# Attention and expert layers on one core: the first pair's loads and start-up work put in another order, and a DMA pipe in the planner's model

## The chip, the core and the metric

The kernel runs on one core of a Trainium2 chip. The core has five engines that run their own instruction lists and wait for each other by semaphores: TensorE (PE, matrix products and transposes), VectorE (DVE), ScalarE (ACT), GpSimd (POOL) and SyncE (SP, which here issues almost all DMA transfers). The metric is the device time of one launch in microseconds (us); less is better. A smaller change of the median than about 0.2% (2.4 us) can't be told from none here.

## The reference, cut to what matters

```python
def _attn_ref(q, k, v):                      # q, k, v: (4, 8, 1152, 64)
    q_pool = q.reshape(B, H, S // 2, 2, D).mean(axis=3)          # 576 pooled rows per head
    scores = scale * np.matmul(q_pool, k.transpose(0, 1, 3, 2))  # 576 x 1152
    scores = scores - np.max(scores, axis=-1, keepdims=True)
    attn = np.exp(scores)
    attn = attn / (np.sum(attn, axis=-1, keepdims=True) + 1e-09)
    return np.matmul(attn, v)

x = attn_out.transpose(0, 2, 1, 3).reshape(2304, 512)
x = ((x @ w1) * (x @ w2) @ w3) @ w_out       # gated layer
logits = x @ w_gate                          # 8 experts; greedy assignment, 288 tokens each
out[mask] = np.maximum(x[mask] @ w1[e], 0.0) @ w2[e]
```

## The kernel before

The kernel has two halves. In the profiled execution the attention fills the first 512 us and the gated layer, the routing of tokens and the experts fill the rest. All products are made in fp32 quality from pairs of fp32r numbers: a value is split into a high part (a cast) and a low part (the value less its high part), and two or three products are summed.

**Tiling of the attention.** Two heads of a batch make a pair; there are 16 pairs. Of each pair the 2 x 576 pooled rows of q are cut into 9 tiles of 128 rows (`tile_ops`, j = 0 to 8): 0 to 3 belong to the first head, 5 to 8 to the second, and tile 4 holds 64 rows of each. For each tile TensorE makes the scores in three pieces of 384 columns (L590, `s<-kst,qst`, two PSUM banks in turn), VectorE copies each piece to SBUF and keeps its minimum (L600, `p<-s`), ScalarE takes the exponential of the whole row (L605), TensorE transposes it back in three groups of three (L614, `pt<-ident,p`), ScalarE or GpSimd makes the high part `p_hi` and VectorE or GpSimd the low part `p_lo`, and `pv` multiplies with v (L664).

**Preparation of a pair.** `prepare_q` loads q (`qr`), adds neighbouring rows (`qs`, L443), transposes and scales (`qT`), splits into `qH` and `qL`, and moves both with eight DMAs inside SBUF to `qst` (`move`, L399). `prepare_k` loads k (`kr`), transposes, splits into `kH` and `kL`, and moves them to `kst`, one buffer for each head. `prepare_v` loads v (`vr`) and splits it (`vhl`). For tile 4 the 64 x 64 blocks `dH` and `dL` stand in for `qst`. For the first pair there is a short way: q is loaded in three groups (`g` 0 to 2), k of the first head is loaded by itself (`k`, L517) and transposed straight into `kst`, and `both` writes half of `qst` without a move.

**What sets the order.** Nothing is issued where it stands in the code. Each step is an `Op` with a cost per engine, a priority and dependences; `Sched.run` plays the whole program through in a model (each engine does the ready op with the lowest priority number next; an op that can run on several engines goes to the one that takes it first) and emits the instructions in order of their model start. The chip then works off each engine's list strictly in that order. A DMA is an op on the queue engine: `dur` is the issue, and `lat` the fixed time from issue to landing. An op's `slack` holds it back for so long after it is ready.

**Before the scheduler.** `routing_consts` makes the constants of the routing (names `rc_...`, needed only after 500 us) straight away: POOL writes number patterns into a spare tile of `xT`, and 27 small DVE instructions make the constants from them. Then `attention` clears parts of `dH` and `dL` with eight DVE memsets (L386, L387). Both stand ahead of everything else in DVE's list.

Of the kernel before, what the change touches and what calls it, by code (L numbers as in the profile page):

```python
# [344 lines left out]
def attention(nc, tc, sch, pool, prep, s_pt, s_s, ident, xT, rsum, q, k, v):  # L345
# [69 lines left out]
    def prepare_q(p, pr):  # L415
# [1440 lines left out]
```

## Time and profile before

| | |
|---|---|
| median of 3 runs | 1190.95 us (1189.04 to 1191.3) |
| the profiled execution | 1188.21 us |
| its span, first to last instruction | 1186.4 us |
| mean granted clock of TensorE | 0.991 of full speed |
| busy share of the span: PE, DVE, ACT, POOL | 97%, 79%, 60%, 44% |

The profiled execution is 2.74 us shorter than the median, and 0.83 us shorter than the fastest of the three runs. Its own time is 1.8 us more than its span. A busy share is a mean over both halves; the attention alone reads differently, as the windows below show.

### The profile page before, as it was taken

The numbers are of one execution on the slowest core, as the hardware profiler recorded it, in microseconds if no ns is written. First come the engines' busy times: TensorE is split into PE (matmuls) and PEld (weight loads), VectorE is DVE, ScalarE is ACT, GpSimd is POOL, SyncE is SP. The second block draws the span as 40 slices with busy tenths as digits, with TensorE's granted clock in tenths as the row PEclk, the third lists the DMA queues.
The fourth block names the chain that finished last, engine by engine and source line by source line (L and its number), as shares of the span: only waits on it lengthen the run. The fifth ranks groups of instructions, "written<-read, shape, count | busy, mean of one in ns | idle before, by whom it ended". The sixth has DMA issues, their size and how long they took to land.

```text
span 1186.4 us, 24411 instructions
## 1 busy us (share of the span) xinstructions
PE 1148.2 (97%) x8401; PEld 1089.1 (92%) x8401; DVE 934.9 (79%) x2955; ACT 706.7 (60%) x1499; POOL 517.0 (44%) x584
## 2 busy tenths in 40 slices
PE   6999999999999999999999999999999899999996
PEld 5999999999999999989999999977778889999996
DVE  7899999999999999998777775468767878877541
ACT  6787888888888888864433344323223455555530
POOL 4466666666656666610000000123444439987110
PEclk9999999999999999999999999999999899999998
DMA  9587676666676654124456660355111565556510
GB/s 215 143 172 156 151 159 145 148 156 157 156 154 149 150 115 106 57 73 155 178 171 193 201 198 22 122 192 171 38 46 45 149 212 182 195 176 198 187 54 21
DMA packets 114539, 168.05 MB, mean 142 GB/s; under 512 B 47543, under 2 KB 77758, under 8 KB 114414
## 3 DMA queue, kind: packets, MB, share of 16 engines
q1 hardware_dynamic: 111246, 157.05, 49.0%
q0 software_dynamic: 3168, 9.44, 2.6%
q8 instruction: 66, 1.08, 0.4%
q14 instruction: 59, 0.48, 0.1%
HBM read 104.87 MB, written 22.61 MB: 107 GB/s over the span
## 4 chain that ended last, share of the span: by engine, by line
PE 83%; DVE 10%; DMA 3%; issue 1%; SPq 1%; ACT 1%; POOL 0%; DVEq 0%; POOLq 0%; ACTq 0%
PE pb L113 40%; PE s L590 13%; PE pt L614 7%; PE pt L664 6%; PE pt L113 6%; PE s L664 6%; PE s L614 4%; DVE pt L113 2%; DMA u<-in_moe_w_dram 1%; DVE ul L113 1%; DVE p L600 1%; PE pt L543 1%; DVE cv_v L113 1%; DVE p_lo L648 0%; PE pt L479 0%
## 5 line engine op out<-in xcount | busy, mean ns | idle before, releaser
L600 DVE TENSOR_SCALAR_CACHE_REDUCE p<-s 128x384 f32<-128x384 f32 x432 | 230.0, 551 | 35.6 <-PE pt L614 12.2
L590 PE MATMUL s<-kst,qst 128*128 128x384 f32 x768 | 200.0, 360 | 6.9 <-DVE p L600 3.4
L605 ACT ACTIVATE p<-p,mn 128x1152 f32<-128x1152 f32 x144 | 181.1, 1258 | 25.2 <-DVE mn L603 23.1
L113 POOL TENSOR_TENSOR x2l<-hraw,x2h 128x512 fp32r<-128x512 f32 x36 | 47.4, 1323 | 291.0 <-PE pt L113 254.3
L113 PE MATMUL pb<-xhi,wh 128*128 128x288 f32 x512 | 155.9, 305 | 1.2 <-ACT wh L113 1.2
L113 PE MATMUL pb<-xhi,wl 128*128 128x288 f32 x512 | 151.0, 295 | 1.4 <-POOL wl L113 1.2
L113 PE MATMUL pb<-xlo,wh 128*128 128x288 f32 x512 | 150.7, 294 | 0.0
L590 PEld LDWEIGHTS s<-kst,qst 128*128 128x128 f32 x768 | 123.8, 191 | 13.1 <-DVE p L600 8.1
L614 PE MATMUL pt<-ident,p 128*128 128x128 f32 x879 | 132.5, 273 | 0.3 <-ACT p L605 0.3
L648 DVE TENSOR_TENSOR p_lo<-pt,p_hi 128x384 fp32r<-128x384 f32 x230 | 124.6, 551 | 0.9 <-ACT p_hi L331 0.9
L331 ACT ACTIVATE p_hi<-pt 128x384 fp32r<-128x384 f32 x230 | 106.6, 493 | 13.5 <-PE pt L614 11.3
L614 PEld LDWEIGHTS pt<-ident,p 128*128 128x128 f32 x879 | 107.3, 141 | 4.3 <-ACT p L605 0.5
L113 PEld LDWEIGHTS pb<-xhi,wh 128*128 128x128 f32 x512 | 96.3, 188 | 2.6 <-ACT wh L113 1.6
L113 PEld LDWEIGHTS pb<-xhi,wl 128*128 128x128 f32 x512 | 96.2, 188 | 1.8 <-POOL wl L113 1.4
L341 POOL TENSOR_TENSOR p_lo<-praw,p_hi 128x384 fp32r<-128x384 f32 x96 | 97.0, 1019 | 0.4
L113 PEld LDWEIGHTS pb<-xlo,wh 128*128 128x128 f32 x512 | 96.3, 188 | 0.0
L113 DVE SCALAR_TENSOR_TENSOR cv_v<-cv_raw,cv_v 128x512 int32<-128x512 int32 (+1 forms) x120 | 83.7, 705 | 5.6 <-ACT cv_raw L113 4.5
L113 POOL TENSOR_TENSOR ul<-u,uh 128x512 fp32r<-128x512 f32 x64 | 81.3, 1300 | 12.0 <-ACT uh L113 10.5
L335 POOL CAST p_hi<-praw 128x384 fp32r<-128x384 f32 x96 | 47.6, 506 | 82.2 <-ACT praw L331 81.9
L113 ACT ACTIVATE uh<-u 128x512 fp32r<-128x512 f32 x128 | 73.7, 625 | 14.7 <-DMA u<-in_moe_w_dram 13.7
L113 PE MATMUL pb<-ehh,uh 128*128 128x288 f32 x256 | 78.6, 307 | 0.0
L113 PE MATMUL pb<-exh,uh 128*128 128x288 f32 x248 | 77.2, 311 | 0.0
(317 smaller groups left out, 3177.4 us busy)
## 6 DMA issues: line engine op xcount, KB each, us to landing
u<-in_moe_w_dram SPq DMA_DIRECT2D x64, 512.0 KB, 3.7
cv_raw<-in_moe_w_dram SPq DMA_DIRECT2D x32, 512.0 KB, 4.0
vr<-in_v_dram SPq DMA_DIRECT2D x32, 288.0 KB, 5.5
kr<-in_k_dram SPq DMA_DIRECT2D x32, 288.0 KB, 5.9
kst<-kH SPq DMA_DIRECT2D x31, 288.0 KB, 4.1
kst<-kL SPq DMA_DIRECT2D x31, 288.0 KB, 5.0
qr<-in_q_dram SPq DMA_DIRECT2D x15, 576.0 KB, 6.3
w3t<-wg SPq DMA_DIRECT2D x16, 512.0 KB, 3.5
```

The source lines that it names most:

```text
L113: return f(*[x.get() if isinstance(x, Lazy) else x for x in a], **{n: x.get() if isinstance(x, Lazy) else x for n, x in k.items()})
L331: nc.scalar.activation(out, in_, AF.Copy)
L335: nc.gpsimd.tensor_copy(out, in_)
L341: (nc.vector if eng == "DVE" else nc.gpsimd).tensor_tensor(out, a, b, op=OP.subtract)
L543: nc.tensor.transpose(ps.tile[:, a * 128:(a + 1) * 128], r[:, 3 * c + a, :, :].rearrange("p h d -> p (h d)"), ident)
L590: nc.tensor.matmul(ps.tile[:, :384], a[:, :], b[:, cs], start=(n == 0), stop=(n == len(passes) - 1))
L600: sch.op("DVE", c_dve(384), lambda ps=ps, c=c, cs=cs: nc.vector.tensor_scalar(t[:, cs], ps.tile[:, :384], 1.0, BIG, op0=OP.mult, op1=OP.mi ...
L605: sch.op("ACT", c_act(S, psum=False, acc=True), lambda: nc.scalar.activation(t, t, AF.Exp, bias=mn[:, 3:4], scale=-1.0, accum_out=sm[0][:, ...
L614: nc.tensor.transpose(ps.tile[:, a * 128:(a + 1) * 128], t[:, b * 128:(b + 1) * 128], ident)
L648: sch.op("DVE", c_dve(384), lambda view=view, src=src: nc.vector.tensor_tensor(view(lo), src(), view(hi).bitcast(F32), op=OP.subtract), us ...
L664: nc.tensor.matmul(ps.tile[:, :n], vt[:, t, :, :], src[half][:, t, off:off + n], start=(half == 0 and t == 0), stop=(half == 1 and t == NT ...
```

## The change

1. `routing_consts` hands its 27 DVE instructions to the scheduler as a chain of ops with priority 60 and a hold of 100 us. The number patterns on POOL stay at the start. `spare_read` keeps the last pair from writing the spare tile ahead of them.
2. The eight memsets of `dH` and `dL` go from DVE to POOL.
3. 14 transposes of the identity into the four `pt` banks stand at the head of PE's list (`WARM`).
4. The loads of `k` and of the first `vr` are issued on ACT's DMA queue, and q group 1 directly after group 0 on SP's.
5. `Sched` gets a `pipe` for the attention's transfers: a transfer lands no earlier than the one before it in the model plus its own size's time, so `lat` is no longer fixed. The first loads' slack now holds too (`pend` starts at `o.slack`), and there are new priorities and costs (`QG1`, `K_FIRST`, `KR_LATE`, `K_PIPE`).

```diff
@@ Sched.op, Sched.run
-    def op(self, engine, dur, fn, r=(), w=(), prio=0.0, lat=None, after=(), takes=None, uses=(), slack=0.0):
+    def op(self, engine, dur, fn, r=(), w=(), prio=0.0, lat=None, after=(), takes=None, uses=(), slack=0.0, pipe=None):
         o = Op()
-        o.slack = slack
+        o.slack, o.pipe = slack, pipe
...
-                    heapq.heappush(pend[e], (0.0, o.idx))
-        t, done = 0.0, 0
+                    heapq.heappush(pend[e], (o.slack, o.idx))
+        t, done, landed = 0.0, 0, 0.0
...
                 end = free[e] = t + o.alts[e]
+                if o.pipe is not None:
+                    landed = max(end + 1200.0, landed) + o.pipe
+                    o.lat = landed + 500.0 - end
@@ attention
-            nc.vector.memset(t[0:64, 64:128].bitcast(F32), 0.0)
-            nc.vector.memset(t[64:128, 0:64].bitcast(F32), 0.0)
+            nc.gpsimd.memset(t[0:64, 64:128].bitcast(F32), 0.0)
+            nc.gpsimd.memset(t[64:128, 0:64].bitcast(F32), 0.0)
...
-        sch.op("DMA", 650, lambda: nc.sync.dma_start(dst.bitcast(F32), src.bitcast(F32)), r=r, w=w, prio=pr, lat=2000)
+        sch.op("DMA", 650, lambda: nc.sync.dma_start(dst.bitcast(F32), src.bitcast(F32)), r=r, w=w, prio=pr, lat=2000, pipe=pipe)
@@ prepare_q
-                   w=[(kq, g) for g in range(3)], prio=pr, lat=3200, slack=SLACK)
+                   w=[(kq, g) for g in range(3)], prio=pr if p > 1 else -4.5, lat=3200, slack=SLACK * (p > 1), pipe=PIPE * 590)
...
-                    w=[(kqs, s_) for s_ in range(slot, slot + 2 * (s1 - s0), 2)], prio=pr)
+                    w=[(kqs, s_) for s_ in range(slot, slot + 2 * (s1 - s0), 2)], prio=(pr, QG1, QD1)[g] if first else pr)
...
-                        "p (s h d) -> p h s d", s=2, h=2)[:, 0], 128, [], key[:2], key[2:], pr + 2 * g + y, -0.0625)
+                        "p (s h d) -> p h s d", s=2, h=2)[:, 0], 128, [], key[:2], key[2:], pr + 0.02 * y, -0.0625)
@@ prepare_k, prepare_v
-            sch.op("DMA", 475, lambda r=r: nc.sync.dma_start(r, dram(k, 0, [[NT * D, 128], [1, NT * D]])), w=[kr], prio=pr, lat=2600)
+            sch.op("ACT", 475, lambda r=r: nc.scalar.dma_start(r, dram(k, 0, [[NT * D, 128], [1, NT * D]])), w=[kr], prio=pr, lat=2600, pipe=PIPE * 295, slack=K_FIRST)
...
-            sch.op("DMA", 475, lambda dst=dst, src=src: nc.sync.dma_start(dst, src), w=[(kr, h)], prio=pr + 2 * h, lat=2600, slack=SLACK)
+            sch.op("DMA", K_LOAD, lambda dst=dst, src=src: nc.sync.dma_start(dst, src), w=[(kr, h)], prio=pr + 2 * h, lat=2600,
+                   slack=SLACK + KR_LATE * (p == 1), pipe=PIPE * 295 * K_PIPE)
...
+        early = p == h == 0
+        sch.op("ACT" if early else "DMA", 475, lambda: (nc.scalar if early else nc.sync).dma_start(
+            r, dram(v, base, [[NT * D, 128], [1, NT * D]])), w=[kr], prio=-88 if early else pr, lat=2600, slack=2 * K_FIRST if early else SLACK, pipe=PIPE * 295)
@@ routing_consts
+    def dve(n, fn):
+        o = sch.op("DVE", c_dve(n), fn, prio=RC_PRIO, lat=0.0, slack=0.0 if made else RC_SLACK)
+        o.deps.update(made[-1:])
+        made.append(o)
...
-    nc.vector.tensor_scalar(tri, jp, 0.0, None, op0=OP.is_le)
+    dve(128, lambda: nc.vector.tensor_scalar(tri, jp, 0.0, None, op0=OP.is_le))
@@
+RC_PRIO, RC_SLACK = 60, 100000.0
+WARM, K_LOAD, KR_LATE = 14, 475, 3000.0
+PIPE, K_PIPE, QG1, K_FIRST = 3.6, 1.4, -3.3, 300.0
@@ attention_moe_experts_kernel
     make_identity(nc, ident)
+    for i in range(WARM):
+        nc.tensor.transpose(pts[i % 4][:, 0:128], ident, ident)
```

The program's order moves on every engine. Three places matter below. First, the head of SP's list. The names are tiles with a buffer number; `kr` is k of both heads of a pair, `vr` is v of a head. Before:

```order
L437 DMA qr_172<-in_q_dram 128x2x256
L517 DMA k_175<-in_k_dram 128x576
L437 DMA qr_172<-in_q_dram 128x2x256
L437 DMA qr_172<-in_q_dram 128x128
L561 DMA vr_176<-in_v_dram 128x576
L534 DMA kr_173<-in_k_dram 128x9x64
L561 DMA vr_177<-in_v_dram 128x576
L534 DMA kr_173<-in_k_dram 128x9x64
L534 DMA kr_174<-in_k_dram 128x9x64 x2
L399 DMA qst_168<-qH_180 64x256 x2
L399 DMA kst_194<-kH_186 64x1152
L399 DMA qst_168<-qH_180 64x256 x2
```

After, the same stretch of SP's list:

```order
L440 DMA qr_159<-in_q_dram 128x2x256 x2
L440 DMA qr_159<-in_q_dram 128x128
L537 DMA kr_160<-in_k_dram 128x9x64
L566 DMA vr_164<-in_v_dram 128x576
L537 DMA kr_160<-in_k_dram 128x9x64
L537 DMA kr_161<-in_k_dram 128x9x64 x2
L435 DMA qr_159<-in_q_dram 128x1152
L402 DMA qst_155<-qH_167 64x256 x2
L402 DMA qst_155<-qL_168 64x256 x2
```

The two loads that SP lost stand ahead of everything else in ACT's list (`k`, then the first `vr`). The load of the second pair's q (L435, 128x1152) came four moves after the loads before (L432); now it is the last of the loads and stands ahead of all moves.

Second, the head of DVE's list. Before, 27 rows of `rc_...` constants and then:

```order
L386 MEMSET dL_185 64x64
L387 MEMSET dL_185 64x64
L443 TENSOR_TENSOR qs_178<-qr_172 128x2x64 x4
L341 TENSOR_TENSOR kst_193<-pt_65,kst_193 64x384
L443 TENSOR_TENSOR qs_178<-qr_172 128x64 x2
L341 TENSOR_TENSOR kst_193<-pt_66,kst_193 64x384
L410 SCALAR_TENSOR_TENSOR qst_168<-pt_67,qst_168 64x128 x4
L341 TENSOR_TENSOR kst_193<-pt_68,kst_193 64x384
L410 SCALAR_TENSOR_TENSOR qst_168<-s_105,qst_168 64x128 x4
L600 TENSOR_SCALAR p_200,mn_198<-s_102 128x384
```

After, from the first row of the list on:

```order
L446 TENSOR_TENSOR qs_165<-qr_159 128x2x64 x2
L413 SCALAR_TENSOR_TENSOR qst_155<-pt_65,qst_155 64x128 x4
L344 TENSOR_TENSOR kst_180<-pt_66,kst_180 64x384
L344 TENSOR_TENSOR kst_180<-pt_67,kst_180 64x384
L344 TENSOR_TENSOR kst_180<-pt_68,kst_180 64x384
L446 TENSOR_TENSOR qs_165<-qr_159 128x2x64 x2
L605 TENSOR_SCALAR p_187,mn_185<-s_116 128x384
L605 TENSOR_SCALAR p_187,mn_185<-s_117 128x384
L446 TENSOR_TENSOR qs_165<-qr_159 128x64 x2
L413 SCALAR_TENSOR_TENSOR qst_155<-s_118,qst_155 64x128 x2
L336 CAST vhl_178<-vr_164 128x9x64
L413 SCALAR_TENSOR_TENSOR qst_155<-s_118,qst_155 64x128 x2
```

The constants now stand between the tiles of the fourth pair, and two score pieces are read before the second group of q is added up and split.

Third, DVE in the middle of the fifth pair, where the next pair's q is prepared. Before:

```order
L600 TENSOR_SCALAR p_201,mn_198<-s_102 128x384
L600 TENSOR_SCALAR p_201,mn_198<-s_103 128x384
L341 TENSOR_TENSOR kL_189<-pt_65,kH_187 128x384
L603 TENSOR_REDUCE mn_198<-mn_198 128x1
L341 TENSOR_TENSOR dL_185<-qT_179,dH_183 64x64 x2
```

After:

```order
L605 TENSOR_SCALAR p_188,mn_185<-s_117 128x384
L336 CAST qH_167<-qT_166 128x4x2x64
L605 TENSOR_SCALAR p_188,mn_185<-s_116 128x384
L344 TENSOR_TENSOR qL_168<-qT_166,qH_167 128x4x2x64
L608 TENSOR_REDUCE mn_185<-mn_185 128x1
L344 TENSOR_TENSOR kL_176<-pt_65,kH_174 128x384
L344 TENSOR_TENSOR dL_172<-qT_166,dH_170 64x64 x2
```

Here `qL` comes to DVE from POOL and `qH` from ACT. Over the whole attention DVE gets 12 more `qL` of this size (13 instead of 1), 7 more `qH` (8 instead of 1) and 8 fewer `qT` (5 instead of 13). From the first products of the gated layer on the order of PE's list is the same but for the places of some small transposes, and its last 4,223 matmuls stand in the same order throughout.

## Rows read from the trace of the kernel before

**Rows 1.** Windows: busy us (instructions) per engine, clock, DMA share, GB/s.
```profile
0.00:15.00 15.00, 8.61 (x40) 6.33 (x40) 11.90 (x61) 8.34 (x23) 7.46 (x22) 1.00 0.84 201
15.00:30.00 15.00, 11.61 (x72) 9.29 (x72) 11.78 (x43) 11.36 (x23) 7.22 (x9) 1.00 1.03 229
...
40.00:50.00 10.00, 8.01 (x46) 7.97 (x47) 6.05 (x23) 5.18 (x11) 4.88 (x6) 0.83 0.56 172
...
70.00:100.00 30.00, 28.13 (x200) 27.43 (x199) 27.11 (x85) 24.24 (x54) 17.45 (x21) 0.95 0.81 179
100.00:505.00 405.00, 404.54 (x2996) 394.56 (x2995) 374.09 (x1239) 350.86 (x756) 256.29 (x286) 1.00 0.61 139
```
**Rows 2.** Waits of PE, 0 to 100 us: total us, times, longest.
```profile
PE pt L526 <- DMA k<-in_k_dram: 4.5, 1, 4.5
PE s L590 <- DVE p L600: 3.4, 4, 1.9
PE s L590 <- DMA qst<-qL: 2.2, 1, 2.2
PE s L590 <- DMA kst<-kL: 1.2, 1, 1.2
```
**Rows 3.** Windows again, the two slow stretches.
```profile
43.00:46.00 3.00, 3.00 (x13) 2.96 (x13) 1.53 (x6) 1.35 (x2) 2.23 (x3) 0.53 0.10 35
...
97.00:100.00 3.00, 3.00 (x15) 3.00 (x14) 2.36 (x7) 1.87 (x6) 2.45 (x4) 0.50 1.03 199
```
**Rows 4.** Timeline of DVE from the start: start, us, instruction, idle before and releaser.
```profile
1.56 0.25 DVE L791 TENSOR_SCALAR rc_tri<-x 128x128 bf16<-128x128 f32 x1 [1.56 <-POOL x L789]
...
4.79 0.18 DVE L847 CAST rc_ids<-x 128x36 bf16<-128x36 int32 x1
...
6.19 0.90 DVE L443 TENSOR_TENSOR qs<-qr 128x128 f32<-128x128 f32 x4
...
8.91 1.23 DVE L410 SCALAR_TENSOR_TENSOR qst<-pt,qst 64x128 fp32r<-64x128 f32 x4 [0.17 <-ACT qT L450]
...
12.00 0.56 DVE L600 TENSOR_SCALAR_CACHE_REDUCE p<-s 128x384 f32<-128x384 f32 x1
```
**Rows 5.** Timeline of DVE, 23 to 45 us: up to the sixth tile's first piece.
```profile
27.91 0.75 DVE L333 CAST vhl<-vr 128x576 fp32r<-128x576 f32 x1 [2.61 <-DMA vr<-in_v_dram]
...
29.05 0.55 DVE L600 TENSOR_SCALAR_CACHE_REDUCE p<-s 128x384 f32<-128x384 f32 x1
```
**Rows 6.** Timeline of SP's DMA issues: the second pair's q, and its last moves.
```profile
15.01 0.54 SPq L432 DMA_DIRECT2D qr<-in_q_dram  x1
...
36.31 2.64 SPq L399 DMA_DIRECT2D qst<-qL  x4
```
**Rows 7.** Timeline of POOL.
```profile
20.90 1.55 POOL L443 TENSOR_TENSOR qs<-qr 128x320 f32<-128x320 f32 x2 [7.18 <-PE s L590]
...
90.86 1.98 POOL L341 TENSOR_TENSOR p_lo<-praw,p_hi 128x384 fp32r<-128x384 f32 x2
92.81 1.14 POOL L443 TENSOR_TENSOR qs<-qr 128x320 f32<-128x320 f32 x2
```
**Rows 8.** Timeline of DVE: instructions with their inputs in SBUF.
```profile
58.87 0.90 DVE L333 CAST qH<-qT 128x512 fp32r<-128x512 f32 x1
...
60.17 1.02 DVE L341 TENSOR_TENSOR qL<-qT,qH 128x512 fp32r<-128x512 f32 x1
...
91.06 2.97 DVE L341 TENSOR_TENSOR dL<-qT,dH 64x64 fp32r<-64x64 f32 x2
```
**Rows 9.** Timeline of PE: its first work, and behind rows 8.
```profile
4.47 1.46 PE L526 MATMUL pt<-ident,k 128*64 128x128 f32 x6 [4.47 <-DMA k<-in_k_dram]
...
63.36 0.62 PE L590 MATMUL s<-kst,qst 128*128 128x384 f32 x2 [0.39 <-DVE p L600]
...
95.61 0.62 PE L590 MATMUL s<-kst,qst 128*128 128x384 f32 x2 [1.87 <-DVE p L600]
```
**Rows 10.** All dL on DVE (duration ns min/median/max), and qT on DVE, 100 to 500 us.
```profile
L341 DVE TENSOR_TENSOR dL<-qT,dH x29: 223/249/2691, 17.0 to 459.8; 64x64 fp32r<-64x64 f32 x29
...
L452 DVE TENSOR_SCALAR qT<-pt 128x512 f32<-128x512 f32 x12 | 8.2, 682 | 0.0
```

More of the change, by code (lines that the diff above doesn't have):

```diff
@@ L159 @@
 class Op:
-    __slots__ = ("alts", "fn", "deps", "prio", "lat", "idx", "takes", "uses", "eng", "pick", "label", "sdeps", "susers", "start", "ready", "readys", "slack", "left", "users")
+    __slots__ = ("alts", "fn", "deps", "prio", "lat", "idx", "takes", "uses", "eng", "pick", "label", "sdeps", "susers", "start", "ready", "readys", "slack", "left", "users", "pipe")
 class Sched:
@@ L396, in split_sbuf, with move @@
                r=list(r) + [kh], w=[kl], prio=pr)
-    def move(dst, src, r, w, pr):
-        sch.op("DMA", 650, lambda: nc.sync.dma_start(dst.bitcast(F32), src.bitcast(F32)), r=r, w=w, prio=pr, lat=2000)
+    def move(dst, src, r, w, pr, pipe):
+        sch.op("DMA", 650, lambda: nc.sync.dma_start(dst.bitcast(F32), src.bitcast(F32)), r=r, w=w, prio=pr, lat=2000, pipe=pipe)
     def both(ps, hi, lo, src, n, r, kh, kl, pr, scale=None):
@@ L506, in prepare_q @@
                 move(dst[rows, x, hs, 256 * y:256 * y + 256], sv[64 * y:64 * y + 64, hs, :], [(ks, 0)],
-                     [(kd, n, y, g, h) for g in range(2) for h in range(2)[hs]], pr)
+                     [(kd, n, y, g, h) for g in range(2) for h in range(2)[hs]], pr, PIPE * (64 if first else 128))
     def prepare_k(p, pr):
@@ L553, in place_k @@
         for x, (t, kt) in enumerate(khl[p]):
-            move(dk[64 * x:64 * x + 64, :], t[64 * h:64 * h + 64, :], [(kt, c, 0) for c in range(3)], [(kdk, x, c) for c in range(3)], pr)
+            move(dk[64 * x:64 * x + 64, :], t[64 * h:64 * h + 64, :], [(kt, c, 0) for c in range(3)], [(kdk, x, c) for c in range(3)], pr, PIPE * 295)
     def prepare_v(p, h, pr):
@@ L773, with routing_consts @@
 NEG = -1e36
-def routing_consts(nc, pool, spare):
+def routing_consts(nc, sch, pool, spare):
     used = [0]
@@ L785, in tmp @@
         return t if len(shape) == 2 else t.rearrange("p (a b) -> p a b", a=shape[1])
-    c = {}
+    c, made = {}, []
+    def dve(n, fn):
+        o = sch.op("DVE", c_dve(n), fn, prio=RC_PRIO, lat=0.0, slack=0.0 if made else RC_SLACK)
+        o.deps.update(made[-1:])
+        made.append(o)
     jp = tmp([128, 128], F32)
@@ L800, in routing_consts @@
     c["rst"] = rst = pool.tile([128, 8, 18], BF16, name="rc_rst")
-    nc.vector.memset(rst, 1.0)
-    nc.vector.memset(rst[:, :, 0:1], 0.0)
+    dve(72, lambda: nc.vector.memset(rst, 1.0))
+    dve(4, lambda: nc.vector.memset(rst[:, :, 0:1], 0.0))
     grid, left = [], 32
@@ L815, in routing_consts, with f @@
     own = tmp([NCG * NTHR, NCG, 8], F32)
-    nc.vector.tensor_scalar(own, v, NTHR - 0.5, None, op0=OP.is_lt)
+    dve(48, lambda: nc.vector.tensor_scalar(own, v, NTHR - 0.5, None, op0=OP.is_lt))
     c["own"] = diag = pool.tile([NCG * NTHR, NCG, 8], BF16, name="rc_diag")
-    nc.vector.scalar_tensor_tensor(diag, v, 0.0, own, op0=OP.is_ge, op1=OP.mult)
+    dve(48, lambda: nc.vector.scalar_tensor_tensor(diag, v, 0.0, own, op0=OP.is_ge, op1=OP.mult))
     u = tmp([NCG * NTHR, NTHR, NCG], F32)
     nc.gpsimd.iota(u, pattern=[[-1, NTHR], [-NTHR, NCG]], base=0, channel_multiplier=1, allow_small_or_imprecise_dtypes=True)
-    nc.vector.tensor_scalar(u, u, 0.0, None, op0=OP.is_equal)
+    dve(90, lambda: nc.vector.tensor_scalar(u, u, 0.0, None, op0=OP.is_equal))
     c["thr"] = sel = pool.tile([NCG * NTHR, NTHR], F16, name="rc_thr")
-    with nc.allow_low_precision(reason="0 or 1"):
-        nc.vector.tensor_reduce(sel, u, axis=AX.X, op=OP.max)
+    def f():
+        with nc.allow_low_precision(reason="0 or 1"):
+            nc.vector.tensor_reduce(sel, u, axis=AX.X, op=OP.max)
+    dve(90, f)
     c["ones16"] = ones16 = pool.tile([98, 128], F16, name="rc_ones16")
-    nc.vector.memset(ones16, 1.0)
+    dve(64, lambda: nc.vector.memset(ones16, 1.0))
     e0 = tmp([128, NTHR, 8], I32)
@@ L853, in routing_consts @@
     nc.gpsimd.iota(row, pattern=[[128, 4]], base=8 * 512, channel_multiplier=1, allow_small_or_imprecise_dtypes=True)
+    c["made"] = made[-1]
     return c
@@ L1818, in attention_moe_experts_kernel @@
     ps_s = [regions["psS"].pool.tile([128, 512], F32, name=f"s{i}") for i in range(4)]
-    rc = routing_consts(nc, G, xT[-1])
+    sch = Sched()
+    sch.label = "attn"
+    rc = routing_consts(nc, sch, G, xT[-1])
     rc["ident"] = ident
     rsum = [dpool.tile([9, 128], F32, name=f"rsum{i}") for i in range(2)]
-    sch = Sched()
     s_pt = Slots(pts)
-    attention(nc, tc, sch, regions["main"].pool, regions["prep"].pool, Slots(pts + ps_s[S_BANKS:]), Slots(ps_s[:S_BANKS]), ident, xT, rsum, q, k, v)
+    attention(nc, tc, sch, regions["main"].pool, regions["prep"].pool, Slots(pts + ps_s[S_BANKS:]), Slots(ps_s[:S_BANKS]), ident, xT, rsum, rc["made"], q, k, v)
     env = {"nc": nc, "G": G, "xT": xT, "main": regions["main"], "prep": regions["prep"], "psS": regions["psS"],
```

42 lines of the change are left out of this document (21 added, 21 removed).

## Prediction, made before the changed kernel had run

> **What bounds the kernel now.** I read the windows first, to find where TensorE (PE) loses time, then PE's waits there, then the timelines of the engines named. From 100 to 505 us PE is busy for 404.54 of 405 us [rows 1]: 7.4 instructions per us, a pair each 30.3 us. A change can take nothing away there; it can only put idle time in. The first 100 us are different. At 7.4 per us the 40 instructions of the first window are 5.4 us of work in 15, the 72 of the second 9.7 in 15, the 46 of 40 to 50 us 6.2 in 10, and the 200 of 70 to 100 us 27.0 in 30 [rows 1]. So PE loses 9.6, 5.3, 3.8 and 3.0 us, 21.7 in all, and that is what the change can win from.
>
> What PE waits for there [rows 2]: the load of `k` (4.5 us, once), the minimum pass `p` on VectorE (DVE; 3.4 us in four waits, the longest 1.9), the second pair's last moves (2.2) and `kst<-kL` (1.2). Two of the waits cost more than their length: behind them the granted clock is 0.53 of 2.4 GHz for 3 us (43 to 46) and 0.50 for 3 us (97 to 100) [rows 3], that is its lower level, and about 1.4 and 1.5 us of work more are lost.
>
> **The change part by part.** *Constants and memsets off DVE's head.* Before, DVE makes constants from 1.56 to 4.97 and clears `dH` and `dL` up to 6.19; only then come the q additions (0.90) and, after more additions and two splits of `qst` (1.23 each), the first score piece at 12.00 [rows 4]. PE's wait for `k` ended at 4.47 [rows 9], and the first q group was issued ahead of `k`, so the additions could start at about 4.4, up to 1.8 us earlier. By the new order half of the additions and one of the two splits also move behind the second piece. The first piece then comes at about 9.9, but the moved half (0.45 + 1.2 us) stands ahead of the third, so that a full row is only some 0.7 us earlier, which is what I count. The eight memsets cost POOL little: it is idle for 7.5 of the first 15 us [rows 1].
>
> *Wait for v.* DVE stands for 2.61 us at 27.91 for a `vr` load of the second pair, with a score piece behind it in its list; the first piece of tile j=5 starts at 29.05 [rows 5]. In the new order the cast of that `vr` isn't in DVE's list at that place (POOL gets it), and the only early cast there is of a load issued with the first ones. 2.6 us go. With the 0.7 before, the **start term is -3.3 us**: tile 5's first piece at about 25.7. Bounds: at least one issue (0.54, [rows 6]) is saved, since `k` no longer queues behind q: -0.5. At most what PE loses in the first window beyond the load, 9.6 - 4.5: -5.
>
> *The second pair's q.* Its load was issued at 15.01, behind moves, POOL began its additions at 20.90 after 7.18 us of idleness, and the last four moves were issued from 36.31 on [rows 6, 7]. PE's 2.2 us and the slow clock behind it (1.4) hang on these, 3.6 in all. Now the load stands ahead of all moves, and POOL can add some 5 us earlier. But with tile 5 earlier by 3.3 PE also comes earlier to the place where it needs them. I take two thirds, **-2.4**; bounds 0 and -3.6.
>
> *The stall at 95 us.* At 91.06 two small `dL` on DVE take 2.97 us; all 29 in the trace have a median of 249 ns, the longest is 2,691 [rows 8, 10]. Over that time POOL runs `p_lo` and then `qs` (from 90.86, 1.98, and 92.81, 1.14 [rows 7]), and PE stands 1.87 us for `p` at 95.61 [rows 9], with the slow clock after it: 1.9 + 1.5 = 3.4 us. Nothing in the change is aimed at it, but all the work around it is placed anew, and one in 29 was so long. Whether another comes in its place I can't read: **-1.5**; bounds 0 and -3.4. The Trainium skill's page "SBUF — State Buffer", section "Who interferes with whom", says that a DVE instruction with both inputs in SBUF contends with a GpSimd instruction that reads SBUF, for whole instructions; the `dL` row agrees with it, since POOL was at work on `p_lo` and `qs` for the whole of its 2.69 us.
>
> *DVE in the steady pairs.* DVE gets 12 more `qL` (1.02 each), 7 more `qH` (0.90), and 8 fewer `qT` (0.682) [rows 8, 10], and the 27 constants (3.4 us, from 1.56 to 4.97, [rows 4]): 12.2 + 6.3 - 5.5 + 3.4 = 16.4 us. From 100 to 505 us DVE is idle for 405 - 374.09 = 30.9 us [rows 1], so it fits on average, at half of the cover. But pieces queue behind a 1 us instruction: behind the only pair with `qH` and `qL` on DVE in the trace, at 58.87 and 60.17, PE stood 0.39 us [rows 8, 9]. 13 such pairs give 5.1 us, the upper bound; 0 the lower, if the new places are where a piece isn't due yet. Between them I take **+2.0**, since ACT and POOL get that work off and PE holds two score banks of reserve.
>
> *Transposes of the identity.* At 0.24 us (1.46 for six of `k`'s, [rows 9]) 14 take 3.4 us; the identity stands before POOL's patterns, which release DVE at 1.56, so they end at about 5.0 and push `k` back by at most 0.5. In the first window the granted clock reads 1.00 [rows 1], so there is nothing to win by warming up either that a row shows. **0**, bounds 0 and +0.5.
>
> *Two queues.* The same bytes come in the same time: the DMA engines are busy for 0.84 and 1.03 of the first two windows, at 201 and 229 GB/s [rows 1]. I count nothing beyond the start term. The Trainium skill's page "DMA: Bandwidth & Descriptors", section "Issuing engines are not separate DMA queues", says that starting transfers from several engines saves only the time to issue them; by that the second queue alone would be worth one issue, about 0.5 us. The shares in rows 1 agree as far as they go.
>
> *All else that is placed anew* (45 to 100 us, the seam at 512 us): **+1.2**; bounds 0 and 1.9, the longest wait for `p` in rows 2.
>
> Sum: -3.3 - 2.4 - 1.5 + 2.0 + 0 + 1.2 = -4.0. The profiled execution took 1188.21, so 1184.2; it lies 2.74 under the median of 1190.95, so on the median's scale **1187.0**.
>
> **The rivals.** *Loads still set the start.* Then the freed DVE waits for q's second group and for v instead, as DMA shares of 0.84 and 1.03 [rows 1] suggest: start term -0.5, the others as above, sum -1.2: 1189.8, no change. Against it: additions start 1.7 us after the data that PE got at 4.47 [rows 4, 9].
>
> *DVE is blocked by POOL.* `qL` has both inputs in SBUF like the `dL` of rows 8, and there are 12 more. If every third pair meets a POOL instruction as that one did, with a stall of 1.9 at PE, or of 2.4 with part of a slow clock, 13/3 x 2.4 = 10.4 us stand in place of 2.0: sum +4.4, **1195.4**, slower. It decides from (4.0 + 2.0)/13 = 0.46 us per pair on, and passes 0.2% at 0.65. For it: `dL`'s one in 29, for instructions a quarter as long, so some one in seven for `qL`; that is half of what it needs.
>
> *More is won.* Start -5, both later stalls gone whole (-3.6, -3.4), DVE +1, the rest +0.5: -10.5, 1180.5.
>
> *The order is no better.* PE's two stalls move by a few us and stay, with start -1.5: -1.5 + 2.0 + 1.2 = +1.7: 1192.7, no change either.
>
> **How the numbers follow.** About 0.2% (2.4 us) is what a measurement here can tell from none. Forecast (gain of 2.4 to 7): 0.43. More is won: 0.15. Loads set the start: 0.15. Order no better: 0.10. DVE blocked: 0.17. Faster is 0.43 + 0.15 = 0.58, within 0.2% 0.25, slower 0.17. The range leaves out a little at each end: 1181 to 1195. The forecast's own range is 1184 to 1188.5.
>
> **What would show it.** In the changed profile: DVE's first instruction is a q addition at 4.4 (over 5.5: loads or the transposes set it); tile 5's first piece at 25.7; no wait of PE on `qst<-qL` over 1 us near 40 and no clock of 0.5 after it; no DVE `dL` or `qL` over 1.5 us; PE idle from 100 to 505 us under 3 us. It is wrong if the first 100 us save less than 4 us, or if PE's waits for `p` in the steady pairs sum to more than 6.

## The result, and the profile after

The changed kernel took 1196.81 us (median of five, 1195.21 to 1200.43) against 1190.95 (1189.04 to 1191.64): a ratio of 1.0058 with an interval of 1.0037 to 1.0078. It is slower by 0.6%, where a gain of 0.3% was forecast, and it lies above the top of the range (1195). The windows say where; the columns are those of [rows 1].

```profile
0.00:15.00 15.00, 10.62 (x42) 7.88 (x42) 7.09 (x23) 6.55 (x19) 7.12 (x28) 0.81 0.89 220
15.00:30.00 15.00, 13.60 (x90) 11.79 (x89) 14.90 (x54) 13.16 (x28) 5.90 (x9) 0.96 0.75 187
...
40.00:50.00 10.00, 10.00 (x73) 9.83 (x72) 9.16 (x29) 8.10 (x17) 5.73 (x8) 1.00 1.00 226
...
70.00:100.00 30.00, 29.28 (x215) 28.08 (x214) 27.53 (x91) 24.88 (x55) 20.14 (x24) 1.00 0.66 155
100.00:505.00 405.00, 399.33 (x2940) 388.05 (x2938) 388.59 (x1269) 341.83 (x731) 248.34 (x275) 1.00 0.59 137
```

From 40 to 100 us PE is fuller than in [rows 1], and the granted clock is 1.00 throughout. From 100 to 505 us it is not: 5.7 us idle where it was 0.5, 56 instructions fewer, and DVE busy 388.59 us where it was 374.09. The main waits of PE (total us, times, longest), first those of 0 to 100 us, then 100 to 512, then 512 to 600:

```profile
PE s L595 <- DVE p L605: 2.6, 3, 1.4
PE s L595 <- DVE kst L344: 2.2, 1, 2.2
...
PE s L595 <- DVE p L605: 4.7, 6, 1.5
...
PE pb L113 <- ACT wh L113: 1.4, 1, 1.4
PE pb L113 <- POOL wl L113: 1.3, 1, 1.3
PE pb L113 <- DVE hraw L113: 1.2, 1, 1.2
```

The waits for `qst<-qL` and `kst<-kL` of [rows 2] are gone, as is the 1.87 us of [rows 9]. New are the 2.2 us for `kst` at the start, waits for `p` in the pairs, and 1.2 us for `hraw`, the first product of the gated layer (before, the waits from 512 to 600 us were 1.2 us for `wh`, 1.2 and 0.2 for `wl`).

The best ruler through the attention is the start of tile 4's first product (`s<-kH,dH`), which each pair has once. The table gives it in us for the pairs 1, 2, 5, 11 and 15, and the start of the last row of `pv` (end of the attention), of the last `wg_hl` and of the last `eo` on DVE (the gated layer, the last expert). Before and after were each profiled a second time (e11, e12). The mean pair is (pair 15 less pair 11) / 4.

| kernel | 1 | 2 | 5 | 11 | 15 | mean pair | last pv | wg_hl | eo |
|---|---|---|---|---|---|---|---|---|---|
| before | 22.92 | 56.28 | 151.20 | 333.46 | 455.47 | 30.50 | 510.62 | 703.67 | 1177.44 |
| before, e11 | 23.69 | 55.31 | 150.49 | 333.54 | 455.65 | 30.53 | 510.81 | 703.81 | 1177.83 |
| after | 23.36 | 53.25 | 146.38 | 333.33 | 456.46 | 30.78 | 512.33 | 707.73 | 1184.45 |
| after, e12 | 22.23 | 52.12 | 145.86 | 333.11 | 456.25 | 30.78 | 512.07 | 707.19 | 1183.76 |
| e2 qL on POOL | 25.05 | 54.93 | 148.39 | 336.24 | 457.77 | 30.38 | 513.59 | 710.11 | 1184.12 |
| e4 before, slack | 23.74 | 54.89 | 147.24 | 331.92 | 455.05 | 30.78 | 510.88 | 706.26 | 1181.44 |
| e5 new start, old engines | 23.08 | 56.44 | 151.63 | 339.26 | 460.60 | 30.34 | 515.76 | 708.88 | 1187.49 |
| e6 old start, new engines | 21.83 | 62.70 | 156.72 | 342.08 | 465.21 | 30.78 | 521.05 | 716.21 | 1193.49 |
| e9 | 23.06 | 57.38 | 148.56 | 330.96 | 452.55 | 30.40 | 508.77 | 699.97 | 1175.44 |
| e14 after, old seam | 22.86 | 52.76 | 146.34 | 333.26 | 456.36 | 30.78 | 512.56 | 705.32 | 1181.06 |

By the means of the two profiles each, the change is 4.7 us ahead at pair 5. It loses 6.2 us from there to the last `pv` (366.1 us against 359.9), 2.2 from there to `wg_hl` (195.3 against 193.0) and 2.7 behind it (476.6 against 473.9): 6.5 us later at the end, against 5.9 between the medians.

### The profile page after: what moved, and what is told of

Its sections match the earlier page's. It is cut to its first block, busy times and chain, and to the rows that moved or that the text cites. A ratio compares the mean times of both kernels' runs of the same rounds, so it can differ in the third digit from the quotient of the medians.

```text
span 1193.4 us, 24489 instructions
## 1 busy us (share of the span) xinstructions
PE 1153.0 (97%) x8415; PEld 1091.6 (91%) x8415; DVE 950.8 (80%) x2971; ACT 703.9 (59%) x1488; POOL 513.1 (43%) x579
## 4 chain that ended last, share of the span: by engine, by line
PE 77%; DVE 14%; issue 4%; DMA 3%; ACT 1%; POOL 1%; SPq 0%; DVEq 0%; POOLq 0%
PE pb L113 40%; PE s L595 11%; PE pt L669 8%; PE pt L113 6%; PE pt L619 6%; PE s L619 4%; DVE p L605 2%; DVE pt L113 2%; DMA u<-in_moe_w_dram 2%; PE s L669 2%; DVE kL L344 1%; DVE dL L344 1%; DVE p_lo L653 1%; DVE ul L113 1%; DVE cv_v L113 0%
## 5 line engine op out<-in xcount | busy, mean ns | idle before, releaser
L619 PE MATMUL pt<-ident,p 128*128 128x128 f32 x819 | 124.7, 272 | 0.0
L653 DVE TENSOR_TENSOR p_lo<-pt,p_hi 128x384 fp32r<-128x384 f32 x217 | 115.4, 549 | 3.9 <-ACT p_hi L334 3.9
L334 ACT ACTIVATE p_hi<-pt 128x384 fp32r<-128x384 f32 x217 | 102.0, 493 | 27.6 <-PE pt L619 24.2
L619 PEld LDWEIGHTS pt<-ident,p 128*128 128x128 f32 x819 | 100.6, 140 | 4.8
L669 PE MATMUL pt<-p_lo,vhl 128*128 128x256 f32 (+1 forms) x468 | 88.4, 304 | 0.0
L669 PE MATMUL pt<-p_hi,vhl 128*128 128x256 f32 (+1 forms) x468 | 83.4, 301 | 0.1
```

What stands on the lines that cost most here:

```text
L334: nc.scalar.activation(out, in_, AF.Copy)
L619: nc.tensor.transpose(ps.tile[:, a * 128:(a + 1) * 128], t[:, b * 128:(b + 1) * 128], ident)
L653: sch.op("DVE", c_dve(384), lambda view=view, src=src: nc.vector.tensor_tensor(view(lo), src(), view(hi).bitcast(F32), op=OP.subtract), us ...
L669: nc.tensor.matmul(ps.tile[:, :n], vt[:, t, :, :], src[half][:, t, off:off + n], start=(half == 0 and t == 0), stop=(half == 1 and t == NT ...
```

## The experiments

Theory D: DVE, with the `qL` and `qH` that the new plan gives it, has become the bound of the steady pairs, and the same kind of shift (`wl` to POOL) costs the seam at 512 us. Theory S: the start is set by the chain of the first pair through DVE and ACT. Theory W: the transposes of the identity bring the slow clock.

**e1, no transposes of the identity.**

```diff
-WARM, K_LOAD, KR_LATE = 14, 475, 3000.0
+WARM, K_LOAD, KR_LATE = 0, 475, 3000.0
```

> The changed kernel without the 14 transposes of the identity; every other instruction in the same order. Theory W (the transposes make TensorE start work at 1.4 us, the gap of 2.2 us behind its first transposes then brings the granted clock down to 0.5 from 9.6 to 16 us): the clock stays at 1.00 over the first 20 us, tile 4 of the first pair comes at 21 us or earlier in place of 23.4, and the time falls by 2 to 3 us to about 1194. Rival (the gap alone brings the clock down, whatever ran before it, or the transposes are hidden beside the loads): slow clock again, within 1 us of 1196.8.

Ratio 1.0071 (1.0052 to 1.0090), not to be told from the change's 1.0058. The clock was as theory W has it. First the changed kernel's windows of 2 us (columns as above), then those of e1:

```profile
8.00:10.00 2.00, 0.98 (x4) 0.80 (x4) 1.94 (x6) 0.58 (x2) 0.29 (x1) 0.83 1.34 228
10.00:12.00 2.00, 2.00 (x7) 0.97 (x5) 1.63 (x8) 0.79 (x3) 0.00 (x0) 0.50 0.93 150
...
14.00:16.00 2.00, 2.00 (x8) 1.68 (x8) 1.96 (x8) 0.89 (x3) 2.00 (x3) 0.50 0.62 193
```

```profile
8.00:10.00 2.00, 0.77 (x2) 0.77 (x3) 1.96 (x5) 0.78 (x3) 0.00 (x0) 1.00 1.34 227
10.00:12.00 2.00, 2.00 (x7) 1.27 (x7) 1.83 (x9) 0.58 (x3) 0.00 (x0) 1.00 0.93 149
...
14.00:16.00 2.00, 1.21 (x9) 0.79 (x8) 1.92 (x9) 0.86 (x4) 1.94 (x3) 1.00 0.66 218
```

But the time did not follow: from 10 to 12 us both do seven PE instructions, and tile 4 of the first pair came at 23.01 against 23.36. PE waits for DVE there at either clock. Theory W's price of 2 to 3 us falls. That the transposes bring the slow clock isn't shown either: e10 below has them, and its clock stays at 1.00.

**e2, the changed order with qL on POOL.**

```diff
-lambda eng: sub(eng, lo, src, hi.bitcast(F32)),
+lambda eng: sub("POOL" if n == 512 else eng, lo, src, hi.bitcast(F32)),
```

> The changed kernel in the same planned order, but the qL splits of 512 columns are given to POOL where they stand (13 leave DVE). Theory D (DVE is the bound of the steady pairs: 30.78 us each from 333 to 456 us against 30.33 before, DVE 96% busy): DVE loses 1.0 us in each of these pairs, pairs return to 30.3 to 30.5 us, the time falls by 4 to 6 us to about 1192. Rival (order of the pieces and moves, not DVE's load): pairs stay at 30.8 and the time at 1196 to 1198, or higher since POOL takes 1.3 us for a qL.

The pairs fell to 30.38 us, as theory D says, in the same order of instructions. The time did not: ratio 1.0072 (1.0054 to 1.0090). PE's waits from 100 to 512 us show why, with a longest of 3.1 us that ends at 218, where the changed kernel had 1.5:

```profile
PE s L595 <- DVE p L605: 5.5, 5, 3.1
PE pt L619 <- DVE p_lo L653: 1.0, 1, 1.0
...
213.78 3.67 DVE L336 CAST dH<-qT 64x64 fp32r<-64x64 f32 x2
```

The last line is what stands on DVE ahead of the late `p`: two small casts, of which one took 3.45 us and the other 0.19. POOL worked from 213.50 to 217.18 without a pause, on `p_hi`, `p_lo` and `qs`. Tile 4 of the first pair was late already, at 25.05 us; why isn't shown.

**e3, a plan in which qL and qH may not go to DVE.**

```diff
-cost = {"DVE": c_dve(n, fast=True), "ACT": c_act(n, False)}
+cost = {"DVE": ..., "ACT": ...} if n < 512 or pr < 0 else {"ACT": c_act(n, False)}
-[("DVE", c_dve(n))] * (DV_LO or pr < 0)
+[("DVE", c_dve(n))] * (n < 512 or pr < 0)
```

> The changed kernel, planned anew with qL and qH of 512 columns forbidden on DVE (POOL and ACT alone). Theory D: pairs of 30.3 us as before the change, with the start kept (4.6 us ahead at 120 us): 1187 to 1190. Rival (the transfers' model or the new start order makes the pairs longer): pairs of 30.7 or more, 1194 or more.

1.0164 (1.0144 to 1.0185), which is neither theory D's time nor a case for the rival: the pairs are uneven (31.3 us on the mean from pair 11 to 15). The planner, left to itself again, made another order with other stalls from 100 to 500 us:

```profile
PE s L595 <- DVE p L605: 6.4, 7, 3.5
PE s L595 <- DMA kst<-kL: 4.8, 4, 2.5
```

**e4, the kernel before with one line of the change.**

```diff
-heapq.heappush(pend[e], (0.0, o.idx))
+heapq.heappush(pend[e], (o.slack, o.idx))
```

> The kernel before with one edit of the change alone: the first loads' slack holds in the planner. No pipe, no transposes, constants at the start. The planner then puts 15 qL and 14 qH on DVE. Theory D: pairs of 30.7 us or more over 200 to 450 us, about 6 us slower than before, 1196 to 1198. Rival (it takes the pipe or the new start to make the pairs longer): pairs of 30.3 us and 1191, give or take 1.5.

1.0060 (1.0038 to 1.0082), with pairs of 30.78 us and 15 `qL` and 14 `qH` on DVE. It is also 3.6 us ahead of before at pair 5, without transposes, second queue, pipe or moved constants. By the table the longer pairs take back just this lead: the attention ends at 510.88 us, where it ended before, and what e4's profile loses lies behind it, 2.4 us up to `wg_hl` and 1.3 after. So one line of planner input turns the whole plan over; among the plans made here in which the planner chose freely, only that of the kernel before has all large `qT` on DVE and `qL` on POOL.

**e5 and e6, start and engines exchanged.** Both kernels have the same operations in the same order of creation, and 56 of the 226 that may go to several engines differ. e5 is the changed kernel with every choice tied to that of before, e6 the kernel before tied to those of the change; each is planned anew.

```diff
+for o, c in zip([o for o in ops if o.pick and len(o.alts) > 1], PICKS):
+    o.alts = {c: o.alts[c]}
```

> The changed kernel, planned as it is, but each of the 226 operations that may go to one of several engines is tied to the engine that it had in the kernel before (56 differ). Theory D (the 13 qL, 8 qH and what follows them on DVE cost 6 to 7 us from 146 to 485 us, and wl on POOL at 512 us 2 us): steady pairs of 30.3 us, no wait for hraw at 530 us, the start's 3 to 4.6 us kept: ratio to before 0.995 to 0.998. Rival (the time of q's preparation in the pair, 17 us later in the planner's model, costs it, not the engine): pairs of 30.7 us, ratio 1.003 or more.

> The kernel before, planned as it is, but with each operation tied to the engine that the changed kernel's plan gave it. Theory D: steady pairs of 30.7 to 30.8 us with DVE 96% busy, the seam as in the changed kernel, no gain at the start: ratio 1.005 to 1.010. Rival: pairs of 30.3 us, ratio within 0.2% of 1.

The steady part follows the engines both ways. Windows from 333 to 456 us of e5 and then e6, columns as above:

```profile
333.00:456.00 123.00, 123.00 (x914) 120.23 (x913) 113.66 (x380) 106.79 (x234) 79.16 (x90) 1.00 0.63 146
```

```profile
333.00:456.00 123.00, 122.44 (x902) 118.77 (x901) 118.16 (x380) 104.21 (x225) 76.53 (x84) 1.00 0.64 149
```

e5 has before's pairs (30.34), e6 has those of the change (30.78). The seam followed too: e5 waits 1.2, 1.2 and 0.2 us there, as before did, and e6 1.7 us for `hraw`, 1.4 for `wl` and 1.4 for `wh`. The whole time followed neither: 1.0104 (1.0088 to 1.0121) and 1.0128 (1.0107 to 1.0149). Choices made for one timeline sit badly in the first eight pairs of another: e6 waits 5.5 us for a `kr` load at 33 us, and e5 is 5.8 us behind by pair 11. The ratios that theory D gave were wrong for both.

**e7 and e8, two parts of the start, one profile each.**

```diff
-RC_PRIO, RC_SLACK = 60, 100000.0
+RC_PRIO, RC_SLACK = -1000, 0.0
```

> The changed kernel with the 27 constants at the head of DVE's list again (priority -1000, no hold); memsets stay on POOL. Only the first 60 us are looked at. Theory S (the first pair's chain through DVE and ACT sets the start: the constants end at about 5.0, 0.6 us after q has landed): tile 4 of the first pair comes 0.5 to 1 us later than 23.4. Rival (constants hidden beside the loads, PE's and ACT's part of the chain sets the time): within 0.3 us of 23.4.

Tile 4 at 23.45 us, though the additions began at 4.94 instead of 4.43: as the rival has it, but the two profiles of the changed kernel (23.36 and 22.23) differ by more than what theory S asked for. e7 was better later, 2.9 us ahead of before in pair 8 where the change was 1.2 ahead, without the 27 constants in the fourth pair; it was planned anew, so that this isn't shown to be the constants alone. In its pairs 5 to 8 PE has no wait for `p`, and no `dL` on DVE took over 0.75 us; both matter below.

```diff
-lambda r=r: nc.scalar.dma_start(r, dram(k, 0, ...))
+lambda r=r: nc.sync.dma_start(r, dram(k, 0, ...))
```

(and the first `vr` likewise)

> The changed kernel with k and the first vr issued on SP's queue again, in the place where the planner puts them (k second, vr fourth). Only the first 60 us are looked at. If the second queue brings something, k lands about 0.5 us later and the first scores, 9.02, come later by as much; if the loads' bytes or DVE set the start, tile 4 of the first pair comes within 0.3 us of 23.4.

Tile 4 at 24.36, 1.0 us later; but the first additions and the first scores (8.27 us in place of 9.02) came earlier, not later. DVE's first instruction in e8, with the wait in front of it; then the same in the changed kernel, followed there by the first, third and sixteenth score piece (the last is tile 5's first):

```profile
3.57 0.49 DVE L446 TENSOR_TENSOR qs<-qr 128x128 f32<-128x128 f32 x2 [3.57 <-DMA qr<-in_q_dram]
```

```profile
4.43 0.49 DVE L446 TENSOR_TENSOR qs<-qr 128x128 f32<-128x128 f32 x2 [4.43 <-DMA qr<-in_q_dram]
...
10.32 0.55 DVE L605 TENSOR_SCALAR_CACHE_REDUCE p<-s 128x384 f32<-128x384 f32 x1
...
14.58 0.56 DVE L605 TENSOR_SCALAR_CACHE_REDUCE p<-s 128x384 f32<-128x384 f32 x1
...
26.97 0.55 DVE L605 TENSOR_SCALAR_CACHE_REDUCE p<-s 128x384 f32<-128x384 f32 x1
```

The first group of q is issued at 0.76 us in both. With `k` behind it on its own queue (at 1.27 us) the additions start 0.86 us earlier than with `k` on the second queue at 0.75 and `vr` and the second group of q at 1.21 and 1.27. Which of the three delays it isn't separated. Since two profiles of the changed kernel differ by 1.1 us at tile 4, e8's 1.0 us there is inconclusive.

**e9 and e10, versions that should keep the lead.** e9 is e4 with `qL` on POOL as in e2, and with the operations from the end of the attention on tied to their old engines. e10 does the same to e7. The tie, where PICKS holds None for all that comes earlier:

```diff
+for o, c in zip([o for o in ops if o.pick and len(o.alts) > 1], PICKS):
+    if c:
+        o.alts = {c: o.alts[c]}
```

> The kernel of e4 (before, with the first loads' slack held in the planner) in its planned order, but the qL of 512 columns are given to POOL where they stand, and the operations from the end of the attention on are tied to the engines that they had before the change. Theory D: steady pairs of 30.4 us in place of 30.8, so that e4's lead of 4 us at 120 us is kept to the end of the attention, and no wait for hraw at 530 us: ratio to before 0.996 to 0.998. Rival (a qL on POOL comes late for its moves, as the longer waits of e2 at 190 to 220 us suggest): new waits for p or qst of 3 us or more, ratio 1.000 or more.

> The changed kernel with the constants at DVE's head as in e7, qL of 512 columns on POOL where they stand, and the end of the attention tied to the old engines. Theory D: e7's lead of 2.9 us at 242 us is kept: ratio 0.997 to 0.999. Rival (POOL's qL late): ratio 1.001 or more.

e9: 0.9979 (0.9966 to 0.9992), the only kernel here that is faster than before. The two largest of its waits of PE from 0 to 100 us, then all of 100 to 512 and of 512 to 600:

```profile
PE pt L540 <- DMA k<-in_k_dram: 4.5, 1, 4.5
PE s L604 <- DMA kst<-kL: 2.7, 1, 2.7
...
PE s L628 <- DVE x L693: 0.3, 1, 0.3
...
PE pb L113 <- DVE wl L113: 1.3, 1, 1.3
PE pb L113 <- ACT wh L113: 0.4, 1, 0.4
```

Pairs of 30.40 us keep the lead: against the mean of before's profiles 2.3 us at pair 5, 3.0 at pair 15, 3.8 at `wg_hl`. e10 came to 1.0005 (0.9991 to 1.0020): a miss for theory D's ratio, while its pairs are 30.38. It has one long wait for `p`, of 2.2 us at 126, and in front of it on DVE

```profile
122.28 3.27 DVE L358 TENSOR_TENSOR dL<-qT,dH 64x64 fp32r<-64x64 f32 x1
```

while POOL worked without a pause up to 125.5 us (`qL`, `qs`, `p_lo`, `qs`). That is the sight of [rows 8] and [rows 7] again.

**e11 and e12, both kernels once more.**

> The kernel before once more, for a second profile: pairs of 30.33 us from 303 to 455 us as in the first, PE's waits at 42 and 95 us again. What differs from the first profile behind 700 us is scatter of the execution: 0 to 4 us.

> The changed kernel once more: pairs of 30.78 us from 333 to 456 us, waits of 1.4, 1.3 and 1.2 us around 515 to 532 us again, the lead over the kernel before at 120 us 4 to 5 us. The slow clock from 9.6 to 16 us may come or not. Behind 700 us scatter of 0 to 4 us.

As expected but for two things. Before's pairs aren't all of 30.33 us: 30.74 and 30.58 occur, so that 30.50 is the mean. And behind `wg_hl` the two kernels' profiles do not scatter over each other: 473.8 and 474.0 us against 476.7 and 476.6. But other kernels with the same lists there scatter as far: e2, which has the changed kernel's order, took 474.0 us, e1 475.1 and e7 479.1.

**e13, the second half of q right behind the first.**

```diff
-PIPE, K_PIPE, QG1, K_FIRST = 3.6, 1.4, -3.3, 300.0
+PIPE, K_PIPE, QG1, K_FIRST = 3.6, 1.4, -89.5, 300.0
```

> The changed kernel, planned anew with the second half of the first pair's q prepared right behind the first (priority -89.5 in place of -3.3). Only the first 30 us are looked at. In the changed kernel the first score piece comes at 10.3 us but the third at 14.3 to 14.6, since the second half of q stands between them. If that place costs the start (theory S), the third piece comes at 13 us or earlier and the first exponential at 14.5 us or earlier, in place of 15.4 to 15.7. Rival (PE's and ACT's part of the chain takes as long in any order): first exponential at 15.2 us or later.

Between the two, nearer to the rival: the third piece at 13.81, with a cast of `vhl` (0.75 us) now ahead of it, the first piece moved back from 10.3 to 12.08, and the first exponential at 15.12.

**e14, the change with the old engines at the seam.** The changed kernel with the tie of e9 and no other edit.

> The changed kernel with the operations from the end of the attention on tied to their old engines, all else planned as in the change. Theory D's second part (wl on POOL costs the seam): no wait for hraw at 530 us, from the last pv to the first sc 88.8 us in place of 90.8, ratio to before 1.003 to 1.005 in place of 1.006. Rival (the seam's order and phase make the waits, not the engine): 90 us or more again, ratio 1.005 to 1.007. From 704 us on all lists are those of before: if the 2.7 us that both profiles of the change lose there come from what goes on before 704, they vary; if 476.6 us come again, it is something that stays.

1.0031 (1.0014 to 1.0048). The waits from 512 to 600 us:

```profile
PE pb L113 <- DVE wl L113: 1.3, 1, 1.3
PE pb L113 <- ACT wh L113: 0.4, 1, 0.4
```

`hraw` is not waited for, and from the last `pv` to `wg_hl` it took 192.8 us in place of 195.3; the first `sc` on DVE still came 90.5 us behind the last `pv`, which the rival had. The six operations that the tie moves at the seam cost 2.5 us. In the table the kernels with the old engines there (before, e5, e9, e14) take 191 to 193 us from the last `pv` to `wg_hl`, those with the new ones 195 to 196.5. Behind `wg_hl` 475.7 us, between the two kernels.

## Why the prediction was wrong

**The steady pairs** are the step that failed: "DVE in the steady pairs", +2.0, with 5.1 as its upper bound. From pair 5 to the end of the attention it cost 6.2 us. The profiles lie 10.5 us above the sum of -4.0: 4.2 of it here, 2.5 in the first five pairs (-4.7 in place of -3.3 - 2.4 - 1.5 = -7.2), and 3.7 in "all else" (2.2 + 2.7 in place of 1.2). The counts were right, and so was 1.02 as the duration of a `qL`. The price was not. It was taken from one wait of PE, 0.39 us, behind one such pair, and the 30.9 us of idle DVE were taken as cover. DVE's groups in the changed kernel from 333 to 456 us (busy us, mean ns, then idle before them):

```profile
L605 DVE TENSOR_SCALAR_CACHE_REDUCE p<-s 128x384 f32<-128x384 f32 x108 | 58.0, 553 | 2.9 <-PE s L619 1.0 <-PE s L595 0.7
L653 DVE TENSOR_TENSOR p_lo<-pt,p_hi 128x384 fp32r<-128x384 f32 x52 | 27.6, 550 | 1.7 <-ACT p_hi L334 1.7
...
L344 DVE TENSOR_TENSOR qL<-qT,qH 128x512 fp32r<-128x512 f32 x4 | 4.1, 1014 | 0.0
L336 DVE CAST qH<-qT 128x512 fp32r<-128x512 f32 x4 | 3.7, 934 | 0.0
```

The same stretch as a window, of the changed kernel and then of before:

```profile
333.00:456.00 123.00, 122.45 (x901) 118.82 (x900) 118.18 (x379) 104.22 (x225) 76.58 (x84) 1.00 0.61 141
```

```profile
333.00:456.00 123.00, 122.83 (x909) 119.36 (x908) 113.94 (x376) 106.52 (x232) 77.68 (x88) 1.00 0.63 142
```

DVE is busy for 118.18 of the 123 us (96.1%), before for 113.94 (92.6%). What is left idle is mainly 4.6 us in four pairs, short gaps in front of `p` and `p_lo` until PE or ACT delivers; since DVE works off its list in order, nothing else fills them. Per pair DVE had 30.50 x 7.4% = 2.26 us idle and has 30.78 x 3.9% = 1.20; its work grew by 1.34 us, of which 1.06 went into gaps and 0.28 made the pair longer. PE shows almost none of it as a wait: it is busy for 122.45 of the 123 us, yet does eight instructions fewer. That `qL` on DVE sets this length is shown by e2 (same order, `qL` away: 30.38), by e5 and e6, and by e4 against e9 (30.78 and 30.40).

The 6.2 us have two parts. e4, with pairs of 30.78 us throughout and no PE wait for `p` above 0.4 us, takes 363.6 us from pair 5 to the last `pv`, 3.7 more than before; e9, which is e4 with `qL` on POOL, takes 360.2. So the longer pairs cost some 3.7 us. The other 2.5 fall between pairs 5 and 8: 94.8 us, where three pairs of 30.78 would take 92.3 (e7 took 92.1). There PE waits for `p` three times, 0.5, 1.0 and 1.5 us. In front of the two longer waits DVE was held in small instructions on `dL` and `dH`. DVE, POOL and PE around the second:

```profile
182.44 2.12 DVE L344 TENSOR_TENSOR dL<-qT,dH 64x64 fp32r<-64x64 f32 x2
...
181.38 1.99 POOL L344 TENSOR_TENSOR p_lo<-praw,p_hi 128x384 fp32r<-128x384 f32 x2
183.33 1.15 POOL L446 TENSOR_TENSOR qs<-qr 128x320 f32<-128x320 f32 x2
...
186.14 0.62 PE L595 MATMUL s<-kst,qst 128*128 128x384 f32 x2 [1.01 <-DVE p L605]
```

The first of the two `dL` took 1.83 us and the second 0.25, a usual value by [rows 10]. Before the third wait a `dH` took 0.94 us and a `dL` 0.95, again beside POOL's `p_lo`.

`qL` itself meets POOL too (duration ns min/median/max, then two of them):

```profile
L344 DVE TENSOR_TENSOR qL<-qT,qH x13: 679/1010/1019, 57.7 to 460.4; 128x512 fp32r<-128x512 f32 x13
...
122.14 0.69 DVE L344 TENSOR_TENSOR qL<-qT,qH 128x512 fp32r<-128x512 f32 x1
...
368.01 1.01 DVE L344 TENSOR_TENSOR qL<-qT,qH 128x512 fp32r<-128x512 f32 x1
```

Five of the 13 took 0.68 to 0.69 us; at three of these POOL was idle, at the others on a cast or on `qs`. Eight took 1.01 to 1.02, each begun while POOL ran `p_lo` (from 366.32 to 368.48 in the last row's case). So about 0.3 us of the 1.34 us of added work per pair stand beside POOL's work, and the 1.02 us of [rows 8], with POOL busy throughout, were such a case already. That POOL causes it is read from this coincidence. No run leaves `qL` on DVE and takes POOL's work away beside it, so that its plain load and its slowing aren't separated.

**"All else", +1.2**, was too small. The seam cost 2.2 us, and e14 shows that the engines of the splits do it. The 2.7 us behind `wg_hl` were not foreseen, and their cause is open. From there on every engine's list is the same, and the waits that differ are of 1 to 2 us for the routing's `rt_own` and `rt_mask`. With these same lists the kernels here took 474 to 479 us, e2 no longer than before, so that the change isn't shown to cost anything there.

**The start term, -3.3.** The first piece of tile 5 came at 26.97 and 25.82 against the 29.05 of [rows 5] and a forecast of 25.7, so the order did most of what was worked out. But PE had no such gain. DVE's wait of 2.61 us for v was counted whole, while PE stood still for only 1.17 + 0.70 us in it and right behind it. With "the second pair's q" (-2.4) the sum had PE 5.7 us earlier in pair 2; by the means of two profiles each it was 3.1 (52.7 against 55.8). And no full row came earlier: the first exponential at 15.72 and 15.41, against 15.58. In e7 and e13, one profile each, neither the constants nor the place of q's second half changed that by more than 0.6 us. Which part of the chain holds it is open.

**The stall at 95 us, -1.5**, measured -1.6 from pair 2 to 5 (93.4 against 95.1 us). The stall isn't chance of one execution: e11 had it again, with a `dL` of 2.97 us. Nothing was aimed at it, and that it shrank (in the changed kernel a `dL` of 1.54 us at 88.31 and a wait of 0.72 at 91.42) is luck of the new placing.

**The transposes, 0**, was right, by e1 within its interval. **Two queues** brought nothing that can be told; the Trainium skill's page "DMA: Bandwidth & Descriptors", section "Issuing engines are not separate DMA queues", has it that such transfers run on the same DMA engines and interleave; e8's 0.86 us agrees, where q came earlier with fewer loads beside it.

**The rivals.** "DVE is blocked by POOL" had the sign, the engine and a part of the mechanism: `dL` and `dH` were held up for some 2.5 us in all, and eight `qL` took 0.3 us longer beside POOL. But no `qL` was held up by 2 us like the `dL` of [rows 8], from which it had its price. Its 0.46 us per pair, from which it decides, is near the 0.5 that the pairs lost (6.2 us in some 12 pairs), most of it by the longer pairs. "The order is no better" was wrong for the first 150 us.

**The signs.** Neither of the two signs of being wrong came: the lead at pair 5 was 4.7 us, and PE's waits for `p` from 100 to 512 us sum to 4.7. They asked for waits of PE, and the loss hardly shows as such. Two of the signs of being right failed: a `dL` took 1.83 us, and PE was idle for 5.7 us from 100 to 505.

## What to carry to other kernels

Idle time of an engine in a loop is cover only as far as its next instruction is ready in it: look at the gaps one by one, and count a long instruction against the gaps that are long enough. When the second engine of a loop is above 90%, price added work at up to its full length, and compare the length of a period, not the waits of the first engine, which read 99.5% busy here while the period grew by 0.9% (30.50 to 30.78 us). Compare the longest and the median duration of small instructions as well: here a `dL` of 1.83 us in place of 0.25 stood in front of a wait of PE. In a kernel whose order a planner makes, a small change of its inputs is a new kernel everywhere: count first which engine gets what in the steady part, and tie what is good there.

## What the runs showed of the hardware

At the start the granted clock differed between kernels that begin alike, and little hung on it. In the changed kernel, after transposes from 1.38 us and a wait of PE of 2.2 us ending at 9.02, it was 0.50, the lower level of 1.2 GHz, from 10 to 16 us. In e12, after the same transposes and a wait of 1.44, it was 0.86 over the first 15 us. In e10, with the transposes and a wait of 1.43 ending at 9.56, it stayed at 1.00:

```profile
10.00:12.00 2.00, 2.00 (x7) 1.46 (x7) 1.99 (x9) 0.27 (x1) 0.00 (x0) 1.00 0.99 159
```

In e1, without them and with a wait of 1.43, it stayed at 1.00 as well. Why isn't shown.

The first additions of q started at 4.43 us (4.37 in e12) with `k`, `vr` and q's second group issued within 0.51 us of its load on two queues, and at 3.57 in e8, with `k` 0.51 us and the second group 1.01 us behind it on one queue.

A DVE instruction with its inputs in SBUF took longer beside some of POOL's: `qL` 1.01 us in place of 0.69, `dL` up to 3.27 (e10) in place of 0.25, and a `dH` cast 3.45 (e2) in place of 0.19, in the last two cases until POOL's run of instructions ended.
